# Scatters of a top-1 expert layer through 40 disjoint views of the output, and a merge that books each kind of transfer

## The chip, the core and the metric

The kernel runs on one core of a Trainium2 chip. The core has five engines that run side by side and meet only through semaphores: PE (TensorE, matrix multiplies; its weight loads are listed as PEld), DVE (VectorE), ACT (ScalarE), POOL (GpSimd) and SP (SyncE, which here only issues transfers). Each engine works through its own instruction list in order; an instruction whose semaphores are not yet there holds up everything behind it on its engine. Transfers (DMA) are issued from SP, POOL or ACT. The metric is the device time of one execution in microseconds (us), less is better.

## The reference, cut to what matters

Attention with a window of 64 positions gives `x` of 4608 tokens by 512. A gate scores each token for 8 experts; each expert takes at most 576 tokens, handed out in the order of the scores. Every expert is a two-layer product over its own tokens:

```
cap = N // E                       # 4608 // 8 = 576
for idx in order:                  # falling scores
    tok, e = (int(idx) // E, int(idx) % E)
    if assigned[tok] >= 0 or counts[e] >= cap:
        continue
    assigned[tok] = e
...
for e in range(E):
    mask = assigned == e
    h = np.maximum(x[mask] @ w1[e], 0.0)
    out[mask] = h @ w2[e]
```

Each token belongs to one expert, so each row of `out` is written once.

## The kernel before, in words

Attention comes first and stores `x` to a buffer `xs` in device memory. Then three things run together for p = 0 to 7, the p-th expert to be settled:

- **Routing** (`Routing.steps`): eight rounds on DVE and PE (line L585 counts, L512 compares) find the expert number `ei` and its threshold. Then `X`, `run`, `Y`, `A`, `B` and `R` on DVE and ACT (half of `R` is made by ACT at L722, the other half by DVE at L728) feed 18 small PE products at L734, and out of these come the token indices `idx` of expert p. Routing p runs while PE computes expert p-1.
- **Weights** (`Experts.load`): eight chunks of 512 KB per expert, four of w1 and four of w2. SP reads `ei` and issues the fetch of a chunk into one of six buffers `st` (L838). ACT rounds it to `wh` (L859) and writes `wl = -wh` (L870); a transfer issued by POOL then adds `st` onto `wl` (L872). The first three chunks of an expert are fetched as soon as `ei` is known.
- **Tokens and products**: POOL gathers the tokens (L913, five pieces `xg`), PE transposes them (L926), ACT and DVE split them into `xh` and `xl` (L903, L907). PE then makes `h` (L972), ACT and DVE turn it into `hh` and `hl` (L944, L949), and PE makes the output tiles `o` (L1004 for the last 64 tokens, L1014 for four tiles of 128). ACT evacuates each into `ot` (L986; for the last 64 tokens into `low`, L989, to which DVE adds the rest, L992), and POOL scatters `ot` to the rows of `out` (L994). There are five scatters per expert, 40 in all.

The order of the instructions on each engine is not written out by hand. `Streams` merges these generators by a simulated clock: each `yield` says how long until the generator may go on, and `busy(dt, eng)` books `dt` nanoseconds on an engine and returns when they end. Two generators that become due at different simulated times are emitted in that order, and what is emitted is the order for good: the chip keeps it on each engine, whatever the real durations are. The lines that decide where `wh` stands among ACT's other work are the estimates of a fetch:

```
SEND = 3400
LOAD = 2600
...
t = max(self.clock(), there.get(i - 1, 0)) + (LOAD if p else 1500) * (1 if i else 2)
```

So for p > 0 the first chunk of an expert is due 5200 ns after its fetch is emitted, and each further one 2600 ns later. A scatter is emitted no earlier than 3400 ns after the one before it (`self.sent + SEND`). The framework sees all scatters write the same tensor `out`, so it makes each scatter wait for the landing of the one before it.

Of the kernel before, what the change touches and what calls it, by code (L numbers as in the profile page):

```python
# [8 lines left out]

FT = mybir.dt.float32  # L10
# [12 lines left out]
E = 8  # L23
# [374 lines left out]
class Routing:  # L398


    def __init__(self, ctx, tc, c, V):
        self.tc, self.nc, self.c, self.V = tc, tc.nc, c, V
        nc = tc.nc
        rt = ctx.enter_context(tc.tile_pool(name="rt", bufs=1))
        self.rt, self.ctx = rt, ctx

        def t(name, shape, dt=FT):
            x = rt.tile(shape, dt, name=name)
            setattr(self, name, x)
            return x  # L410

        for name in ("eid", "un", "m", "best"):
            t(name, [128, NJ])
        for name in ("oh", "w", "one"):
            t(name, [128, NJ, E], BF)
        t("G0", [128, NJ, ND], BF)
        t("cw", [128, E])
        t("dg", [128, ND], I32)
        t("lane", [128, 1])
        t("rows", [128, 1], U32)  # L420
        self.setup = self.constants(c["jp"], t)
        self.idx, self.eint = {}, {}
# [367 lines left out]
STAGE = 6  # L790

GATHER = (2900, 6500)
SEND = 3400
LOAD = 2600
ADDED = 4500
FIRST = 6500

# [1 line left out]
class Experts:  # L799
    def __init__(self, ctx, tc, c, xs, w1, w2, out, ring=8):  # L800
        self.tc, self.nc, self.c = tc, tc.nc, c
        self.xs, self.w1, self.w2, self.out = xs, w1, w2, out
        self.ring = ring
        self.fw = ctx.enter_context(tc.tile_pool(name="fw", bufs=1))
        self.ps = ctx.enter_context(tc.tile_pool(name="fp", bufs=1, space=PSUM))
        self.W = {}
        self.XT = {}
        self.used = 0
        self.taken = 0
        self.first = 0  # L810
        self.gathered = 0
        self.sent = 0
        self.turned = 0
        self.tiles = [0] * E
        self.lows = [0] * E
# [10 lines left out]
    def load(self, p, ei):  # L826

        nc, fw = self.nc, self.fw
        yield lambda: self.taken == 2 * NCH * p
        e = nc.sync.value_load(ei[0:1, 0:1], min_val=0, max_val=E - 1)  # L830
        eg = nc.gpsimd.value_load(ei[0:1, 0:1], min_val=0, max_val=E - 1) if p == 0 else None
        st, there = {}, {}

        def fetch(i):
            st[i] = fw.tile([128, 1024], FT, name="st", bufs=STAGE)

            q, r = (nc.gpsimd, eg) if p == 0 and i >= 4 else (nc.sync, e)
            q.dma_start(st[i], self.part(i, r))  # L838

            t = max(self.clock(), there.get(i - 1, 0)) + (LOAD if p else 1500) * (1 if i else 2)  # L840
            if p == 0 and i == 4:

                t = max(t, self.clock() + self.busy(0, "pool") + FIRST)
            there[i] = t

        ahead = 3 if p else 4
        for i in range(ahead):
            fetch(i)
        if p == 0:
            yield lambda: self.gathered  # L850
        for i in range(2 * NCH):
            if p == 0 and i == 3:
                yield lambda: self.tiles[0] > 1
            yield lambda: self.taken - self.ring < self.used
            if there[i] > self.clock():
                yield there[i] - self.clock()
            hi = fw.tile([128, 1024], FR, name="wh", bufs=self.ring)
            lo = fw.tile([128, 1024], FR, name="wl", bufs=self.ring)
            nc.scalar.activation(hi, st[i], AF.Copy)  # L859
            yield 1050  # L860
            quick = self.quick(p, i)
            if not (p and quick):
                yield lambda: self.gathered > p
            if quick:
                nc.vector.tensor_tensor(lo, st[i], hi.bitcast(FT), OP.subtract)  # L865
                dt = self.busy(1130, "dve")
                self.spawn(self.ready(p, i, hi, lo), dt + 300 if p else 0)
            else:

                nc.scalar.activation(lo, hi.bitcast(FT), AF.Copy, scale=-1.0)  # L870
                yield 1150
                nc.gpsimd.dma_start(lo.bitcast(FT), st[i], accum_op=OP.add)  # L872
                self.spawn(self.ready(p, i, hi, lo), self.busy(650, "pool") + ADDED - 1200)
                dt = 1300
            self.taken += 1
            if i + ahead < 2 * NCH:
                fetch(i + ahead)
            yield max(100, dt - 1200) if p or i < 3 else 900
# [16 lines left out]
    def turn(self, p, idx):  # L895

        nc, fw = self.nc, self.fw
        yield lambda: self.turned == p

        def evac(a, n, t):  # L900
            r = slice(128 * a, 128 * a + n)
            t = t.bitcast(FT)
            nc.scalar.activation(xh[:, :, r], t[:, :, :n], AF.Copy)  # L903
            self.tiles[p] = a + 1
            yield 700
            self.busy(600, "dve")
            nc.vector.tensor_tensor(xl[:, :, r], t[:, :, :n], xh[:, :, r].bitcast(FT), OP.subtract)  # L907
            self.lows[p] = a + 1

        g = fw.tile([128, 5, DM], FT, name="xg")  # L910
        for a in range(5):
            n = 128 if a < 4 else 64
            nc.gpsimd.indirect_dma_start(out=g[0:n, a], out_offset=None, in_=self.xs,  # L913
                                         in_offset=IndirectOffsetOnAxis(ap=idx[0:n, a:a + 1], axis=0))
        self.gathered += 1
        there = self.clock() + self.busy(6400, "pool") + GATHER[p > 0]
        yield lambda: self.first == p
        xh = fw.tile([128, NX, CAP], FR, name="xh")
        xl = fw.tile([128, NX, CAP], FR, name="xl")
        self.XT[p] = (xh, xl)  # L920
        for a in range(5):
            n = 128 if a < 4 else 64
            yield max(0, there - 1280 * (4 - a) - self.clock())
            t = self.ps.tile([128, NX, 128], FR, name="tp", bufs=2)
            for cc in range(NX):
                nc.tensor.transpose(t[:, cc, :n], g[0:n, a, 128 * cc:128 * cc + 128].bitcast(FR), self.c["identr"][0:n, 0:n])  # L926
            dt = self.busy(300)
            self.spawn(evac(a, n, t), dt + 150)
            if p == 0 and a < 1:
                self.warm(6)  # L930
            yield dt + (1000 if p else 600)
        yield 1500
        self.turned += 1

    def steps(self, p, idx):
        nc, fw = self.nc, self.fw
# [45 lines left out]
        def put(a, o):  # L982
            ot = fw.tile([128, DM], FT, name="ot", bufs=3)
            m = 128 if a < 4 else 64
            if a < 4:
                nc.scalar.activation(ot, o, AF.Copy)  # L986
            else:
                t = fw.tile([64, DM], FT, name="low")
                nc.scalar.activation(t, o[64:128], AF.Copy)  # L989
                yield 650  # L990
                self.busy(600, "dve")
                nc.vector.tensor_tensor(ot[0:64], o[0:64], t, OP.add)  # L992
            yield max(600, self.sent + SEND - self.clock())
            nc.gpsimd.indirect_dma_start(out=self.out,  # L994
                                         out_offset=IndirectOffsetOnAxis(ap=idx[0:m, a:a + 1], axis=0),
                                         in_=ot[0:m], in_offset=None)
            self.sent = self.clock() + self.busy(1040, "pool")


        o = self.ps.tile([128, DM], FT, name="o", bufs=2)  # L1000
        for f in range(NF):
            yield lambda: (p, NCH + f // 2) in self.W
            for n, w in enumerate(self.W[p, NCH + f // 2]):
                nc.tensor.matmul(o, hh[:, f, 512:], w[:, 512 * (f % 2):512 * (f % 2) + 512],  # L1004
                                 start=(f == 0 and n == 0), stop=(f == NF - 1 and n == 1))
                yield self.busy(228)
        self.spawn(put(4, o), 100)
        for a in range(4):
            o = self.ps.tile([128, DM], FT, name="o", bufs=2)
            k = 0  # L1010
            for f in range(NF):
                wh, wl = self.W[p, NCH + f // 2]
                for wt, ht in ((wh, hh), (wl, hh), (wh, hl)):
                    nc.tensor.matmul(o, ht[:, f, 128 * a:128 * a + 128], wt[:, 512 * (f % 2):512 * (f % 2) + 512],  # L1014
                                     start=(k == 0), stop=(k == 23))
                    k += 1
                    yield self.busy(228)
            self.spawn(put(a, o), 100)
# [95 lines left out]
```

## Time and profile before

| | |
|---|---|
| median of 3 runs | 655.87 us (655.83 to 656.62) |
| the profiled execution's own time | 653.74 us |
| its span in the trace | 652.1 us |
| PE busy | 620.3 us, 95% of the span |
| weight loads busy (PEld) | 534.1 us, 82% |
| DVE, ACT, POOL busy | 447.3, 346.4, 187.6 us |

The span runs from the first to the last instruction of the program. A PE that is shown busy nearly all the time is either doing useful work or holding matmuls whose records overlap; whether it loses time is read from its waits and from the distance between the starts of its instructions. The trace belongs to one execution, which was 2.13 us quicker than the median of the timed runs.

### The profile page before, as it was taken

What the parts mean: (1) busy time and instruction counts of PE and PEld (TensorE: products, weight loads), DVE (VectorE), ACT (ScalarE), POOL (GpSimd) and SP (SyncE); (2) the same over time, 40 slices, a digit from 0 to 9 for tenths busy, and PEclk for the clock granted to TensorE, in tenths of its full rate; (3) what the DMA queues carried; (4) which work ended last, traced back from release to release, by engine and by line L of the source; (5) the groups of instructions that cost most, each with busy time, mean ns of one, the idle gap of its engine ahead of it and who ended that gap; (6) DMA issues with size and microseconds to landing.
All of it is one profiled execution on the core that took longest, in us unless ns stands there. A gap on an engine that the chain in (4) does not pass through costs nothing.

```text
span 652.1 us, 16839 instructions
## 1 busy us (share of the span) xinstructions
PE 620.3 (95%) x6383; PEld 534.1 (82%) x6383; DVE 447.3 (69%) x2102; ACT 346.4 (53%) x721; POOL 187.6 (29%) x234
## 2 busy tenths in 40 slices
PE   8999999994599999999999999999999999999996
PEld 6777778874488779978988898799889879989985
DVE  7988888887787757866885886688578754523310
ACT  6898999980254176246517624561744364424210
POOL 1333253330151062125306022430612154011011
PEclk9999999996599999999999999999999999999999
DMA  9999999921476197669739776964977599301001
GB/s 311 363 365 368 370 385 378 347 88 36 146 222 127 31 320 191 122 221 215 186 70 301 188 146 222 222 157 104 286 191 146 198 213 323 132 28 45 1 25 48
DMA packets 44656, 127.80 MB, mean 196 GB/s; under 512 B 4632, under 2 KB 5272, under 8 KB 44576
## 3 DMA queue, kind: packets, MB, share of 16 engines
q1 hardware_dynamic: 30736, 79.52, 33.9%
q0 software_dynamic: 13552, 46.69, 31.0%
q8 instruction: 50, 0.82, 0.5%
q10 hardware_dynamic: 288, 0.52, 0.3%
q14 instruction: 30, 0.25, 0.1%
HBM read 82.15 MB, written 18.87 MB: 155 GB/s over the span
## 4 chain that ended last, share of the span: by engine, by line
PE 65%; issue 5%; DVE 4%; DMA 2%; ACT 1%; POOLq 0%; ACTq 0%
PE h L972 29%; PE o L1014 26%; PE o L1004 3%; PE rps L585 2%; PE tp L926 2%; DMA st<-w 2%; PE rps L734 1%; PE rps L519 1%; DVE hl L949 1%; DMA out<-ot,idx 0%; ACT hh L944 0%; DVE run L693 0%; DVE sq L594 0%; DVE X L676 0%; DVE wl L865 0%
## 5 line engine op out<-in xcount | busy, mean ns | idle before, releaser
L994 POOL DMA_INDIRECT out<-ot,idx x40 | 42.1, 1051 | 300.2 <-DVE ot L992 110.6
L944 ACT ACTIVATE hh<-h 128x256 fp32r<-128x256 f32 (+1 forms) x128 | 52.5, 410 | 111.3 <-PE h L972 110.2
L1014 PE MATMUL o<-wh,hh 128*128 128x512 f32 x256 | 102.5, 400 | 0.0
L1014 PE MATMUL o<-wl,hh 128*128 128x512 f32 x256 | 101.8, 398 | 0.0
L1014 PE MATMUL o<-wh,hl 128*128 128x512 f32 x256 | 101.4, 396 | 0.0
L949 DVE SCALAR_TENSOR_TENSOR hl<-h,hh 128x256 fp32r<-128x256 f32 x128 | 53.4, 417 | 61.3 <-ACT hh L944 60.4
L140 ACT ACTIVATE pe<-st,mx 128x128 f32<-128x128 f32 x288 | 91.9, 393 | 5.8 <-DVE mx L135 5.5
L972 PE MATMUL h<-xh,wl 128*128 128x256 f32 (+1 forms) x512 | 93.0, 299 | 0.0
L972 PE MATMUL h<-xh,wh 128*128 128x256 f32 (+1 forms) x512 | 91.9, 299 | 0.7 <-ACT xh L903 0.7
L972 PE MATMUL h<-xl,wh 128*128 128x256 f32 (+1 forms) x512 | 92.0, 298 | 0.4 <-DVE xl L907 0.4
L972 PEld LDWEIGHTS h<-xh,wh 128*128 128x128 f32 x512 | 75.9, 189 | 1.6 <-ACT xh L903 0.8
L972 PEld LDWEIGHTS h<-xh,wl 128*128 128x128 f32 x512 | 76.1, 189 | 0.2
L972 PEld LDWEIGHTS h<-xl,wh 128*128 128x128 f32 x512 | 75.7, 190 | 0.7 <-DVE xl L907 0.6
L859 ACT ACTIVATE wh<-st 128x1024 fp32r<-128x1024 f32 x64 | 67.2, 1050 | 3.4 <-DMA st<-w 3.4
L135 DVE CUSTOM_DVE_ANT_0 st<-Sp,mask 128x128 f32<-128x128 f32 x288 | 63.8, 285 | 7.0 <-PE Sp L127 6.6
L986 ACT ACTIVATE ot<-o 128x512 f32<-128x512 f32 x32 | 19.2, 599 | 82.3 <-PE o L1014 80.9
L1014 PEld LDWEIGHTS o<-wh,hl 128*128 128x128 f32 x256 | 48.1, 188 | 9.4 <-issue 0.4
L1014 PEld LDWEIGHTS o<-wh,hh 128*128 128x128 f32 x256 | 48.2, 188 | 8.9
L1014 PEld LDWEIGHTS o<-wl,hh 128*128 128x128 f32 x256 | 48.2, 188 | 8.6
L913 POOL DMA_INDIRECT xg<-xs,idx x40 | 41.9, 1046 | 44.8 <-DVE eq L755 34.5
L870 ACT ACTIVATE wl<-wh 128x1024 fp32r<-128x1024 f32 x49 | 51.8, 1057 | 0.7
L872 POOL DMA_DIRECT2D wl<-st x49 | 45.8, 1278 | 14.5 <-ACT wl L870 14.5
(178 smaller groups left out, 1098.5 us busy)
## 6 DMA issues: line engine op xcount, KB each, us to landing
st<-w SPq DMA_DIRECT2D x60, 512.0 KB, 6.8
wl<-st POOLq DMA_DIRECT2D x49, 512.0 KB, 7.7
xs<-x SPq DMA_DIRECT2D x36, 256.0 KB, 5.1
VO<-v SPq DMA_DIRECT2D x6, 1168.0 KB, 17.8
Q<-q SPq DMA_DIRECT2D x6, 1152.0 KB, 14.1
K<-k SPq DMA_DIRECT2D x6, 1152.0 KB, 16.0
VT<-vt SPq DMA_DIRECT2D x6, 1152.0 KB, 16.0
VO<-v SPq DMA_DIRECT2D x4, 584.0 KB, 7.9
```

The lines of the kernel that those rows point to most:

```text
L135: nc.vector.tensor_tensor_reduce(st[:, h, :], Sp[h % 2][:, h // 2], mk, scale=-0.125, scalar=3.0e38, op0=OP.add, op1=OP.min, accum_out=mx[ ...
L140: nc.scalar.activation(pe[:, h, :], st[:, h, :], AF.Exp, bias=mx[:, h:h + 1], scale=-1.0)
L859: nc.scalar.activation(hi, st[i], AF.Copy)
L870: nc.scalar.activation(lo, hi.bitcast(FT), AF.Copy, scale=-1.0)
L872: nc.gpsimd.dma_start(lo.bitcast(FT), st[i], accum_op=OP.add)
L913: nc.gpsimd.indirect_dma_start(out=g[0:n, a], out_offset=None, in_=self.xs, in_offset=IndirectOffsetOnAxis(ap=idx[0:n, a:a + 1], axis=0))
L944: nc.scalar.activation(hh[:, f, c0:c1], h, AF.Relu)
L949: nc.vector.scalar_tensor_tensor(t, h[:, a - c0:b - c0], 0.0, hh[:, f, a:b].bitcast(FT), op0=OP.max, op1=OP.subtract)
L972: nc.tensor.matmul(h, wv[:, cc, 128 * (f % 2):128 * (f % 2) + 128], xt[:, cc, c0:c1], start=(k == 0), stop=(k == 11))
L994: nc.gpsimd.indirect_dma_start(out=self.out, out_offset=IndirectOffsetOnAxis(ap=idx[0:m, a:a + 1], axis=0), in_=ot[0:m], in_offset=None)
L1004: nc.tensor.matmul(o, hh[:, f, 512:], w[:, 512 * (f % 2):512 * (f % 2) + 512], start=(f == 0 and n == 0), stop=(f == NF - 1 and n == 1))
L1014: nc.tensor.matmul(o, ht[:, f, 128 * a:128 * a + 128], wt[:, 512 * (f % 2):512 * (f % 2) + 512], start=(k == 0), stop=(k == 23))
```

## The change

Three edits. The output is cut into 40 views over the same bytes, one for each scatter, which the framework takes as tensors that do not overlap, so that scatters no longer wait for one another. In the merge, the transfers become one more engine, `"dma"`: a fetch books 1350 ns (`PLAIN`), an adding transfer 2650 (`ADDING`), a gather or scatter 700 (`TOKENS`), and a transfer is due `LAND` = 2000 ns behind the end of its booking. The spacing of 3400 ns between scatters goes.

```diff
-SEND = 3400
-LOAD = 2600
+PLAIN, ADDING, TOKENS, LAND = 1350, 2650, 700, 2000
...
-        self.xs, self.w1, self.w2, self.out = xs, w1, w2, out
+        self.xs, self.w1, self.w2 = xs, w1, w2
+
+        self.out = dram_disjoint_views(out, 5 * E)
...
-            t = max(self.clock(), there.get(i - 1, 0)) + (LOAD if p else 1500) * (1 if i else 2)
+            t = self.clock() + self.busy(PLAIN, "dma") + LAND
+            if p == 0:
+                t = max(self.clock(), there.get(i - 1, 0)) + 1500 * (1 if i else 2)
...
-                self.spawn(self.ready(p, i, hi, lo), self.busy(650, "pool") + ADDED - 1200)
+                t = self.busy(650, "pool")
+                t = max(t + 350 + ADDING, self.busy(ADDING, "dma")) + LAND if p else t + ADDED - 1200
+                self.spawn(self.ready(p, i, hi, lo), t)
...
                                          in_offset=IndirectOffsetOnAxis(ap=idx[0:n, a:a + 1], axis=0))
+            self.busy(TOKENS, "dma")
...
-            yield max(600, self.sent + SEND - self.clock())
-            nc.gpsimd.indirect_dma_start(out=self.out,
+            yield max(600, self.sent - self.clock())
+            nc.gpsimd.indirect_dma_start(out=self.out[5 * p + a],
...
                                          in_=ot[0:m], in_offset=None)
+            self.busy(TOKENS, "dma")
```

`dram_disjoint_views` belongs to the framework: it returns as many handles on one tensor as it is asked for, between which no dependencies are kept.

The order of PE's and of SP's instructions stays as it was, row for row. DVE's differs only in the last two experts, where a few `wl` and `hl` of L865 and L949 change places. ACT's and POOL's change from expert 1 on. The changed kernel's line numbers are a little higher: `wh` is L863 there, `wl` L874 on ACT and L876 on POOL, `R` L723, `low` L996, `ot` L993, `hh` L951 and the scatter L1001.

POOL, during the output tiles of expert 0, behind the first three adding transfers of expert 1 (chunks 0 to 2), with the semaphores that each row waits for (DMASW: transfers issued by POOL, eight in turn; DMAHW: fetches of SP). Before:

```order
L872 DMA wl<-st 128x1024 [waits DMASW2_49,DMAHW6_49,PE_49,Activation_49]
L994 DMA out<-ot,idx_3991 4608x512 [waits DMASW7_49,DMASW3_49,Activation_49]
L994 DMA out<-ot,idx_3991 4608x512 [waits DMASW4_49,DMASW3_49,Activation_49]
L872 DMA wl<-st 128x1024 [waits DMASW5_49,DMAHW7_49,PE_49,Activation_49]
L872 DMA wl<-st 128x1024 [waits DMASW6_49,DMAHW0_49,PE_49,Activation_49]
```

And now:

```order
L1001 DMA out<-ot,idx_3991 4608x512 [waits DMASW2_49,Activation_49]
L876 DMA wl<-st 128x1024 [waits DMASW3_49,DMAHW6_49,PE_49,Activation_49]
L1001 DMA out<-ot,idx_3991 4608x512 [waits DMASW4_49,Activation_49]
L876 DMA wl<-st 128x1024 [waits DMASW5_49,DMAHW7_49,PE_49,Activation_49]
L876 DMA wl<-st 128x1024 [waits DMASW6_49,DMAHW0_49,PE_49,Activation_49]
```

Each scatter has lost the one wait that was for the scatter before it and keeps the wait for the eighth transfer back; one adding transfer now stands behind a scatter instead of ahead of it.

ACT, in the `h` products of expert 1, around the last two chunks of its weights (chunks 6 and 7). Before:

```order
L870 ACTIVATE wl<-wh 128x1024
L859 ACTIVATE wh<-st 128x1024
L944 ACTIVATE hh<-h 128x320
L870 ACTIVATE wl<-wh 128x1024
L859 ACTIVATE wh<-st 128x1024
L944 ACTIVATE hh<-h 128x320
L870 ACTIVATE wl<-wh 128x1024
L944 ACTIVATE hh<-h 128x320
```

And now:

```order
L874 ACTIVATE wl<-wh 128x1024
L951 ACTIVATE hh<-h 128x320
L863 ACTIVATE wh<-st 128x1024
L951 ACTIVATE hh<-h 128x320
L874 ACTIVATE wl<-wh 128x1024
L951 ACTIVATE hh<-h 128x320
L951 ACTIVATE hh<-h 128x256
L863 ACTIVATE wh<-st 128x1024
L874 ACTIVATE wl<-wh 128x1024
```

Chunk 6 moves behind one `hh`, chunk 7 behind two more.

ACT, where the output tiles of expert 2 begin and routing 3 ends; the `wh` is chunk 0 of expert 3. Before:

```order
L944 ACTIVATE hh<-h 128x320
L989 ACTIVATE low<-o 64x512
L722 ACTIVATE R<-A,lane 128x18x18x2
L859 ACTIVATE wh<-st 128x1024
L986 ACTIVATE ot<-o 128x512
```

And now:

```order
L951 ACTIVATE hh<-h 128x320
L996 ACTIVATE low<-o 64x512
L863 ACTIVATE wh<-st 128x1024
L723 ACTIVATE R<-A,lane 128x18x18x2
L993 ACTIVATE ot<-o 128x512
```

The same place for chunk 0 of expert 5 (and in the same way of expert 6), where `low`, `R`, `wh` stood before, now reads:

```order
L951 ACTIVATE hh<-h 128x320
L863 ACTIVATE wh<-st 128x1024
L996 ACTIVATE low<-o 64x512
L723 ACTIVATE R<-A,lane 128x18x18x2
L874 ACTIVATE wl<-wh 128x1024
```

For experts 2, 3 and 4 `wh` has moved ahead of `R` and stands behind `low`; for experts 5 and 6 it has moved ahead of `low` as well. Between the `xh` of each expert there now stand the `wh` and `wl` of its chunk 3, which stood ahead of them.

## Rows read from the trace of the kernel before

**Rows 1.** The page, busy us of each engine, share of the span, instructions.
```profile
PE 620.3 (95%) x6383; PEld 534.1 (82%) x6383; DVE 447.3 (69%) x2102; ACT 346.4 (53%) x721; POOL 187.6 (29%) x234
```

**Rows 2.** Busy us by stretch: PE, PEld, DVE, ACT, POOL, then clock, DMA.
```profile
344.12:401.23 57.11, 57.00 (x424) 50.40 (x423) 43.47 (x177) 29.57 (x48) 18.10 (x18) 1.00 0.73 193
```

**Rows 3.** PE's waits, whole span, then 240:652 us: total, times, longest us.
```profile
PE rps L734 <- ACT R L722: 2.7, 1, 2.7
PE rps L585 <- DVE G L512: 0.3, 1, 0.3
```

**Rows 4.** POOL's timeline: start, us, what, [idle before <- who ended it].
```profile
257.74 1.01 POOL L994 DMA_INDIRECT out<-ot,idx  x1 [11.57 <-DMA out<-ot,idx]
```

**Rows 5.** Chain that ended last, 246 to 262 us: start, us, what.
```profile
247.15 9.96 DMA st<-w
258.11 0.43 ACT hh L944
```

**Rows 6.** PE's timeline, 258 to 260.3 us, around the first L585 that waits.
```profile
258.80 0.40 PE L972 MATMUL h<-xh,wl 128*128 128x256 f32 x2
259.55 0.59 PE L585 MATMUL rps<-G,one 128*128 128x60 bf16 x9 [0.35 <-DVE G L512]
```

**Rows 7.** SP's timeline: fetch issue of chunk 0 of experts 2 to 6.
```profile
282.14 0.34 SPq L838 DMA_DIRECT2D st<-w  x1
339.52 0.34 SPq L838 DMA_DIRECT2D st<-w  x1
396.14 0.34 SPq L838 DMA_DIRECT2D st<-w  x1
453.20 0.34 SPq L838 DMA_DIRECT2D st<-w  x1
511.93 0.34 SPq L838 DMA_DIRECT2D st<-w  x1
```

**Rows 8.** Those fetches: size, us from issue to landing; experts 2, then 3, then 5.
```profile
st<-w SPq DMA_DIRECT2D x1, 512.0 KB, 4.0
st<-w SPq DMA_DIRECT2D x1, 512.0 KB, 3.7
st<-w SPq DMA_DIRECT2D x1, 512.0 KB, 3.6
```

**Rows 9.** ACT's timeline: expert 1's xg stage, then the end of routing 3.
```profile
237.09 1.05 ACT L859 ACTIVATE wh<-st 128x1024 fp32r<-128x1024 f32 x1
238.04 1.32 ACT L553 COPY one<-one 128x384 bf16<-128x384 bf16 x3
242.08 0.60 ACT L903 ACTIVATE xh<-tp 128x512 fp32r<-128x512 f32 x1 [0.73 <-PE tp L926]
342.19 0.90 ACT L722 ACTIVATE R<-A,lane 128x648 bf16<-128x648 bf16 x1 [2.64 <-DVE A L720]
343.24 1.06 ACT L859 ACTIVATE wh<-st 128x1024 fp32r<-128x1024 f32 x1 [0.15 <-DMA st<-w]
```

**Rows 10.** PE's timeline: first matmuls of L734, routings 2 to 6.
```profile
287.19 1.24 PE L734 MATMUL rps<-B,R 128*72 128x64 bf16 x18
343.96 1.24 PE L734 MATMUL rps<-B,R 128*72 128x64 bf16 x18
401.06 1.12 PE L734 MATMUL rps<-B,R 128*72 128x64 bf16 x16
458.79 1.24 PE L734 MATMUL rps<-B,R 128*72 128x64 bf16 x18
517.22 1.24 PE L734 MATMUL rps<-B,R 128*72 128x64 bf16 x18
```

**Rows 11.** ACT's low, DVE's ot and DVE's half of R, routing 5.
```profile
456.27 0.60 ACT L989 ACTIVATE low<-o 64x512 f32<-64x512 f32 x1 [3.91 <-PE o L1004]
456.90 0.68 DVE L992 TENSOR_TENSOR ot<-o,low 64x512 f32<-64x512 f32 x1
457.51 0.73 DVE L728 TENSOR_TENSOR R<-A,row 128x648 bf16<-128x648 bf16 x1
```

More of the change, by code (lines that the diff above doesn't have):

```diff
@@ L7 @@
 from concourse import mybir
+from concourse.ap import dram_disjoint_views
 from concourse.bass import IndirectOffsetOnAxis, ds
```

## The prediction

> **What bounds the kernel now.** I read the page first, then the stretches, then PE's waits. PE is busy 95% of the span [rows 1]. In the stretch of one expert it is busy 57.00 of 57.11 us at the full clock, 1.00, while DVE, ACT and POOL stay at 76% or less [rows 2]. PE's waits say the same from the other side: after 240 us only one wait of PE is listed, 0.3 us before a counting product of the routing [rows 3]. So from expert 1 on the kernel runs at the pace of PE's own list, and the change leaves that list as it was, row for row. It can only take away what PE still waits for, which is little, or make PE wait for something that is in time today.
>
> That PE can be made to wait for `R` is seen in routing 0, where it stood 2.7 us for ACT's `R` at L734 [rows 3]. In routings 2 to 6 it does not.
>
> **The scatters.** The wait that goes is real on POOL: one scatter of expert 0 stood 11.57 us for the landing of the one before it, with four adding transfers queued behind [rows 4]. But no wait of PE after 240 us names an adding transfer, a gather or a scatter [rows 3]. I cost the freed POOL queue at nothing; what it could give at most is the next point.
>
> **The one wait that goes.** Around 247 us the fetch of chunk 7 of expert 1 takes 9.96 us, ACT stands for it with an `hh` queued behind, which starts at 258.11 [rows 5], DVE waits for this `hh`, and the comparison for L585 stands behind it on DVE. PE shows 0.35 us idle; counted from the start of the second matmul ahead of it, since records overlap, up to 0.6 [rows 6]. In the new order chunk 6 stands one `hh` later and chunk 7 two more, so ACT does not hold these `hh` for the fetch. I take -0.5 us, between 0.35 and 0.6.
>
> **The wait that comes.** For p > 0 the first chunk of an expert was due 5.2 us after its fetch by the merge's clock; now it is due 1.35 + 2.0 = 3.35 us after. That is why `wh` of chunk 0 has moved ahead of `R` for experts 2 to 6. ACT works in order, so `R` is now late by whatever the fetch is late. The fetch goes out when `ei` is known, at the times of [rows 7], and lands 3.6 to 4.0 us later [rows 8]: later than booked. In the old order this hurt nobody: for expert 3 `R` ran at 342.19, and `wh` started at 343.24, held 0.15 us by the landing [rows 9].
>
> Now expert by expert. ACT starts `wh` 0.02 us behind the landing; an independent activation behind a `wh` starts 0.95 us after it (237.09 to 238.04), and `R` takes 0.90 [rows 9]. PE stood ready for L734 at the times of [rows 10].
>
> - Expert 3: `wh` 343.24, `R` 344.19 to 345.09, PE ready 343.96: PE waits 1.13.
> - Expert 2: landing 282.14 + 4.0 = 286.14, `R` ends 286.16 + 0.95 + 0.90 = 288.01, PE ready 287.19: 0.82.
> - Expert 4, with the 3.7 of expert 3: 396.14 + 3.7 + 0.02 + 1.85 = 401.71, PE ready 401.06: 0.65.
> - Expert 5: `wh` stands ahead of `low` too, and DVE's list has `ot` (L992), which needs `low`, ahead of its own half of `R` (L728). Today `low` takes 0.60, `ot` starts 0.03 after it, L728 starts 0.61 after that and takes 0.73 [rows 11]. `wh` 453.20 + 3.6 + 0.02 = 456.82, `low` 457.77 to 458.37, `ot` 458.40, L728 459.01 to 459.74, PE ready 458.79: 0.95.
> - Expert 6 in the same way, with 3.7: `wh` 515.65, `low` ends 517.20, L728 ends 518.57, PE ready 517.22: 1.35.
>
> Together 4.90 us. These waits add up: PE has nothing else to do in them, because its list is in order, and after each the whole rest slides, the routing of the next expert with it, so that `ei`, fetch and L734 keep their distances. Experts 1 and 7 keep `R` where it was.
>
> The Trainium skill, "DMA: Bandwidth & Descriptors", section "Anatomy of one DMA — SWDGE (gpsimd) path", fits a transfer as 2.0 us plus its bytes over 436 GB/s. For 512 KB that gives an estimate of 3.2 us, less than the trace's 3.6 to 4.0 [rows 8]; with 3.2 in all five places the waits would be 2.2 us in place of 4.9, and the time 657.6 us. The fit is for one transfer from POOL, while these fetches come from SP in bursts, so I stay with the rows.
>
> **The rest of ACT.** Chunk 3's `wh` and `wl` now stand between the `xh`. A `wh` is 1.05 us and the idle time before an `xh` is 0.73 [rows 9], so an `xh` can come up to 0.32 late, in six experts at most 1.9 us. The other bound is nothing: the transposes have two buffers and PE does other products between them. I take nothing, since PE lists no wait for `xh` after 240 us [rows 3]. The changed order of DVE in the last two experts is covered in the same way: PE lists no wait for a `wl` or an `hl` there [rows 3]; uncovered, I let it share the bound just given.
>
> **Sum.** 4.90 - 0.5 = +4.4 us. The profiled execution would go from 653.74 to 658.1 us and its span from 652.1 to 656.5. The median of the runs shown is 2.13 us above the profiled execution; I add the change to it: 655.87 + 4.4 = 660.3 us.
>
> **The rivals.** What a measurement of this kernel can tell from no change is about 0.2%, 1.3 us.
>
> - *Shorter landing.* The fetch lands as the merge books it, 3.35 us after issue. For it: the fetches of chunks 1 and 2 go out right behind the first and share its way, so 3.6 to 4.0 need not be a floor. Against: the burst is the same in the new kernel. The five waits shrink by 0.65, 0.35, 0.35, 0.25 and 0.35, to 2.95; with -0.5 the time is 658.3 us. The skill's fit, above, goes the same way, and its 657.6 us belongs to this case. Chance 0.06.
> - *Hidden after all (not slower).* PE reaches L734 later, or the fetch goes out earlier, so that `R` is in time behind `wh`. It decides at a landing 1.85 us and a little before PE's time, for expert 3 at 342.1, which is 2.6 us after issue. Nothing in rows 8 comes near. What could speak for it is a routing that gains on PE once DVE no longer waits for `hh`; against it, each of the eight rounds waits for L585 in PE's own order. It gives 655.87 - 0.5 = 655.4 us. Chance 0.07.
> - *Faster.* The early scatters and adding transfers free buffers and the DMA engines, and PE gains more than its listed waits. Everything listed after 240 us is the 0.3 to 0.6 us of above; to pass 1.3 us the distances between its matmuls would have to shrink too. 655.87 - 1.5 = 654.4 us. Chance 0.03.
> - *More waits.* The `xh` term comes in full: 4.9 + 1.9 - 0.5, 662.2 us, or more. Chance 0.04.
>
> **How the numbers follow.** The forecast, five waits of 0.6 to 1.4 us at L734 less one of 0.5, has 0.80; its own range is 659.2 to 661.6 us. Reaching to the shorter landing on one side (657.6) and to the full `xh` term on the other (662.2) leaves out the two cases at or under 655.4 and little else: 657.4 to 662.2 us. Slower has 0.80 + 0.06 + 0.04 = 0.90, within 0.2% 0.07, faster 0.03.
>
> **What would show it.** PE's waits of the changed kernel should list L734 waiting for ACT's `R` (routings 2, 3, 4) and for DVE's L728 (routings 5, 6), together near 4.9 us. ACT's timeline should show `wh` of chunk 0 ended by the landing of `st`, with `R` right behind it, and idle ACT ahead of it. The L585 near 259.5 us should have no wait, and POOL's scatters no wait for a scatter. I am wrong if L734 shows no wait, if landings fall under 3 us, or if PE's waits stand somewhere else, above all at the transposes.

## The result, and the profile after

The changed kernel takes 660.25 us (median of 6 runs, 659.17 to 661.5), the kernel before, beside it, 655.85 us (6 runs, 655.6 to 656.62). The ratio is 1.0073, with an interval of 1.0051 to 1.0094: slower by 3.3 to 6.2 us. The profiled execution took 659.17 us, with a span of 657.5 us; before it was 653.74 and 652.1.

The page of the changed kernel, busy time by engine, and from its costliest groups the rounding of weights: out and in, count, busy us and mean ns of one, idle us before and what ended it.

```profile
PE 620.2 (94%) x6383; PEld 533.5 (81%) x6383; DVE 447.9 (68%) x2102; ACT 346.0 (53%) x721; POOL 185.4 (28%) x234
...
L863 ACT ACTIVATE wh<-st 128x1024 fp32r<-128x1024 f32 x64 | 67.3, 1052 | 22.1 <-DMA st<-w 22.0
```

PE, DVE and ACT are busy for the same time as in [rows 1], within 0.6 us; PE 620.2 us where it was 620.3. So the 5.4 us between the two spans are not work: they are time in which PE stands idle. The page's one loud line is misleading about where: ACT stands 22 us for fetches ahead of `wh`. Idle time of ACT costs nothing in itself, so the question is how much of it PE sees.

PE's waits of the changed kernel, 240 to 658 us (total, times, longest, in us):

```profile
PE rps L735 <- DVE R L729: 2.8, 2, 1.5
PE rps L735 <- ACT R L723: 1.6, 3, 0.8
```

Five waits at one place, where [rows 3] has none after 240 us, and the L585 wait of 0.3 us gone. For the same time ACT's list of waits has 19.4 us at `wh`, in five pieces of up to 5.0 us, where before it had 0.8 (before, then changed):

```profile
ACT wh L859 <- DMA st<-w: 0.8, 2, 0.7
...
ACT wh L863 <- DMA st<-w: 19.4, 5, 5.0
```

PE sees 4.4 us of them.

The stretch in the middle of the span (columns as in [rows 2]):

```profile
344.00:401.00 57.00, 56.10 (x417) 49.41 (x416) 42.60 (x177) 29.07 (x46) 16.42 (x18) 1.00 0.71 187
```

PE is idle 0.90 us of 57.00, at full clock, where [rows 2] has 0.11. The five places on PE's timeline: the last product of the output tile ahead, then the first of the 18 products (start, us, what, idle before and who ended it).

```profile
287.08 0.39 PE L1022 MATMUL o<-wh,hl 128*128 128x512 f32 x1
287.85 0.89 PE L735 MATMUL rps<-B,R 128*72 128x64 bf16 x12 [0.38 <-ACT R L723]
...
344.41 0.39 PE L1022 MATMUL o<-wh,hl 128*128 128x512 f32 x1
345.59 0.65 PE L735 MATMUL rps<-B,R 128*72 128x64 bf16 x8 [0.79 <-ACT R L723]
...
402.43 0.39 PE L1022 MATMUL o<-wh,hh 128*128 128x512 f32 x1
403.29 0.89 PE L735 MATMUL rps<-B,R 128*72 128x64 bf16 x12 [0.48 <-ACT R L723]
...
460.90 0.39 PE L1022 MATMUL o<-wh,hl 128*128 128x512 f32 x1
462.59 1.24 PE L735 MATMUL rps<-B,R 128*72 128x64 bf16 x18 [1.30 <-DVE R L729]
...
520.72 0.39 PE L1022 MATMUL o<-wh,hl 128*128 128x512 f32 x1
522.65 1.24 PE L735 MATMUL rps<-B,R 128*72 128x64 bf16 x18 [1.54 <-DVE R L729]
```

The number in brackets is too small, because a record of 0.39 us overlaps the next one: where L735 does not wait, it starts 0.23 us after such a product (shown under e9 below). Counted from starts, less 0.23, PE loses 0.54, 0.95, 0.63, 1.46 and 1.70 us, together 5.28.

Why it waits is on ACT's timeline, at expert 3 and at expert 5:

```profile
339.62 0.60 ACT L996 ACTIVATE low<-o 64x512 f32<-64x512 f32 x1 [3.60 <-PE o L1012]
343.72 1.06 ACT L863 ACTIVATE wh<-st 128x1024 fp32r<-128x1024 f32 x1 [3.50 <-DMA st<-w]
344.69 0.85 ACT L723 ACTIVATE R<-A,lane 128x648 bf16<-128x648 bf16 x1
...
459.39 1.06 ACT L863 ACTIVATE wh<-st 128x1024 fp32r<-128x1024 f32 x1 [4.69 <-DMA st<-w]
460.48 0.60 ACT L996 ACTIVATE low<-o 64x512 f32<-64x512 f32 x1
460.97 0.87 ACT L723 ACTIVATE R<-A,lane 128x648 bf16<-128x648 bf16 x1
```

and on DVE's, at expert 5:

```profile
461.11 0.68 DVE L999 TENSOR_TENSOR ot<-o,low 64x512 f32<-64x512 f32 x1 [1.99 <-ACT low L996]
461.71 0.72 DVE L729 TENSOR_TENSOR R<-A,row 128x648 bf16<-128x648 bf16 x1
```

For expert 3, ACT stands 3.50 us with nothing to do but wait for the fetch, while `R` is queued behind it; in [rows 9] `R` had run at 342.19. For expert 5 the wait goes through one engine more: `low` stands behind `wh` on ACT, DVE stands 1.99 us for `low`, and its half of `R` is queued behind that.

With that the two spans can be compared: 5.28 us lost at L735, 0.66 gained near 259 us (below), and 0.79 that was there before any row changed place (the first L734 of routing 1 starts at 229.67 us before and L735 at 230.45 after; one execution against another). 5.28 - 0.66 + 0.79 = 5.4 us, and 5.4 lie between the spans.

The gain is real too. PE near 259 us, the place of [rows 6]: first the product that follows L585 there before, then the same place of the changed kernel:

```profile
259.97 0.48 PE L972 MATMUL h<-xh,wl 128*128 128x256 f32 x2
...
259.58 0.40 PE L979 MATMUL h<-xh,wl 128*128 128x256 f32 x2
259.83 0.43 PE L586 MATMUL rps<-G,one 128*128 128x60 bf16 x9
260.09 0.48 PE L979 MATMUL h<-xh,wl 128*128 128x256 f32 x2
```

No wait, and 0.25 us between the first two starts where [rows 6] has 0.75: 0.5 us. The next product starts 0.26 us after L586, where it was 0.42 after L585: 0.16 more, 0.66 together. And the scatter of [rows 4] now waits 4.04 us for its data and no longer 11.57 for another scatter:

```profile
249.90 1.05 POOL L1001 DMA_INDIRECT out<-ot,idx  x1 [4.04 <-ACT ot L993]
```

### The profile page after: what moved, and what is told of

Read it like the earlier page. It is cut to its first block, busy times and chain, and to the rows that moved or that the text cites. A ratio compares the mean times of both kernels' runs of the same rounds, so it can differ in the third digit from the quotient of the medians.

```text
span 657.5 us, 16849 instructions
## 1 busy us (share of the span) xinstructions
PE 620.2 (94%) x6383; PEld 533.5 (81%) x6383; DVE 447.9 (68%) x2102; ACT 346.0 (53%) x721; POOL 185.4 (28%) x234
## 4 chain that ended last, share of the span: by engine, by line
PE 46%; issue 19%; DVE 4%; DMA 4%; ACT 2%; POOL 1%; SPq 0%; POOLq 0%; ACTq 0%
PE h L979 21%; PE o L1022 18%; DMA st<-w 3%; PE rps L586 2%; PE tp L933 2%; PE rps L735 1%; POOL out L1001 1%; PE o L1012 1%; DMA xg<-xs,idx 1%; DVE hl L956 1%; ACT R L723 1%; ACT wh L863 0%; ACT hh L951 0%; ACT low L996 0%; DVE sq L595 0%
## 5 line engine op out<-in xcount | busy, mean ns | idle before, releaser
L1001 POOL DMA_INDIRECT out<-ot,idx x40 | 41.6, 1040 | 262.4 <-DVE ot L999 122.1
L951 ACT ACTIVATE hh<-h 128x256 fp32r<-128x256 f32 (+1 forms) x128 | 52.5, 410 | 110.2 <-PE h L979 109.1
L863 ACT ACTIVATE wh<-st 128x1024 fp32r<-128x1024 f32 x64 | 67.3, 1052 | 22.1 <-DMA st<-w 22.0
L993 ACT ACTIVATE ot<-o 128x512 f32<-128x512 f32 x32 | 19.2, 599 | 90.6 <-PE o L1022 88.6
L876 POOL DMA_DIRECT2D wl<-st x49 | 44.9, 978 | 57.3 <-ACT wl L874 37.5
L874 ACT ACTIVATE wl<-wh 128x1024 fp32r<-128x1024 f32 x49 | 51.7, 1055 | 0.5
```

What stands on the lines that cost most here:

```text
L951: nc.scalar.activation(hh[:, f, c0:c1], h, AF.Relu)
L1001: nc.gpsimd.indirect_dma_start(out=self.out[5 * p + a], out_offset=IndirectOffsetOnAxis(ap=idx[0:m, a:a + 1], axis=0), in_=ot[0:m], in_off ...
```

## The experiments

The theory: `wh` of chunk 0 stands ahead of `R` (and of `low`) on ACT and is held by a fetch that lands later than booked; PE waits for `R` at L735, five times, and apart from the half microsecond near 259 us nothing else of the change moves the time. The rivals to it were that the views or the earlier scatters cost or gain something themselves, that the other moved rows (`xh`, `hh`, chunks 6 and 7) matter, and that it is the place of `wh` that costs, its own 1 us on ACT, whatever the fetch does. The medians of the kernel before beside these runs were 656.72 us (e1, e2, e3, e5), 654.89 (e4, e6, e7, e8) and 655.24 (e9, e10).

### The two halves apart: e1_views_only, e2_merge_only

The kernel before with nothing but the 40 views:

```diff
-        self.xs, self.w1, self.w2, self.out = xs, w1, w2, out
+        self.xs, self.w1, self.w2, self.out = xs, w1, w2, dram_disjoint_views(out, 5 * E)
...
-            nc.gpsimd.indirect_dma_start(out=self.out,
+            nc.gpsimd.indirect_dma_start(out=self.out[5 * p + a],
```

> The kernel before, with only the 40 views: the order of every engine is that of before, row for row, and only the waits of scatters for scatters are gone. Theory (the loss comes from wh of chunk 0 standing ahead of R): no L734 waits after 240 us, 655.4 to 656.4 us, the same as before. Rival (earlier scatters and adding transfers collide with the fetches): a good part of the loss of 4.4 us is here already, 658 us or more.

Measured: 657.15 us, ratio 1.0009 (0.9992 to 1.0026). PE's waits, 240 to 660 us:

```profile
PE rps L586 <- DVE G L513: 0.6, 1, 0.6
PE h L973 <- ACT hh L945: 0.5, 1, 0.5
PE h L973 <- DVE hl L950: 0.4, 1, 0.4
PE tp L927 <- DVE xl L908: 0.3, 1, 0.3
```

and its POOL near 250 us:

```profile
250.03 1.01 POOL L995 DMA_INDIRECT out<-ot,idx  x1 [4.02 <-ACT ot L987]
```

The scatter is free of its 11.57 us, the time is the same as that of the kernel before beside it (656.72 us; both lie above the range expected in microseconds), the L585 wait (L586 here) is still there. That the changed kernel has no such wait comes from the merge, not from the views.

The changed kernel with one output tensor, the merge alone:

```diff
-        self.out = dram_disjoint_views(out, 5 * E)
+        self.out = out
...
-            nc.gpsimd.indirect_dma_start(out=self.out[5 * p + a],
+            nc.gpsimd.indirect_dma_start(out=self.out,
```

> The changed kernel, with one output tensor again: the order is that of the changed kernel, and scatters wait for scatters. Theory: the five waits at L734 stay, near 4.9 us together, and the time is 659.5 to 661.5 us; the POOL queue, though held up by scatters again, adds nothing since PE waits for nothing from it. Rival (the released traffic makes the loss): back to about 656 us.

Measured: 661.58 us, ratio 1.0084 (1.0067 to 1.0102). PE's waits after 215 us:

```profile
PE rps L735 <- DVE R L729: 2.5, 2, 1.5
PE rps L735 <- ACT R L723: 2.0, 3, 1.1
```

The whole loss is in the merge. The median stands 0.1 us above the range that was expected; the last section has what else was seen in this trace.

### One number of the merge: e3_first_late, e5_before_early

The changed kernel with chunk 0 booked 1850 ns later, as late as it was due before:

```diff
-            t = self.clock() + self.busy(PLAIN, "dma") + LAND
+            t = self.clock() + self.busy(PLAIN, "dma") + LAND + (1850 if i == 0 else 0)
```

> The changed kernel, with the estimate of the first chunk of an expert alone put back to 5.2 us: low, R and wh stand in the old order, everything else as in the changed kernel. Theory: all five waits at L734 go, the stall near 259 us stays away, 655.0 to 655.9 us. Rival (the rest of ACT's new order, wh and wl between the xh above all): most of the loss stays, 658 us or more.

Measured: 655.81 us, ratio 0.9996 (0.9976 to 1.0016). No wait at L735. ACT at expert 3:

```profile
342.43 0.90 ACT L723 ACTIVATE R<-A,lane 128x648 bf16<-128x648 bf16 x1 [2.63 <-DVE A L721]
...
343.43 1.06 ACT L863 ACTIVATE wh<-st 128x1024 fp32r<-128x1024 f32 x1
```

`R` is ahead again, no wait at L586 is listed either, and the loss is gone, with the views, the freed scatters and the other new bookings still in place.

The other way round, the kernel before with chunk 0 due 1850 ns earlier and chunk 1 kept where it was:

```diff
+            if p and i == 0:
+                t -= 1850
+            if p and i == 1:
+                t += 1850
```

> The kernel before, with the estimate of the first chunk of an expert alone cut to 3.35 us (the second is left where it was): low, wh and R stand as in the changed kernel, the scatters wait and are spaced as before. Theory: five waits at L734 of 4.9 us together, the stall near 259 us stays, 660.3 to 661.2 us. Rival (the views or the rest of the merge make the loss): 656 us.

Measured: 662.6 us, ratio 1.011 (1.0082 to 1.0137). PE's waits after 215 us:

```profile
PE rps L734 <- DVE R L728: 2.7, 2, 1.4
PE rps L734 <- ACT R L722: 2.1, 3, 1.0
PE rps L585 <- DVE G L512: 0.3, 1, 0.3
```

This one number makes the loss by itself. It is 5.9 us above the kernel before beside it, more than the change cost and more than was expected; the last section has what else was seen in its trace.

### The dose: e6_early_5_6, e7_early_2_4, e4_first_early

The changed kernel with chunk 0 early for experts 5 and 6 alone (e6, late for p < 5), or for 2 to 4 alone (e7, late for p > 4):

```diff
-            t = self.clock() + self.busy(PLAIN, "dma") + LAND
+            t = self.clock() + self.busy(PLAIN, "dma") + LAND + (1850 if i == 0 and p < 5 else 0)
...
+            t = self.clock() + self.busy(PLAIN, "dma") + LAND + (1850 if i == 0 and p > 4 else 0)
```

> The changed kernel, with the estimate of the first chunk put back to 5.2 us for experts 1 to 4 alone, so that wh stands ahead of low and R for experts 5 and 6 only. Theory (the waits are separate and add up): the two waits for DVE's half of R stay, 2.3 to 3.0 us together, and those for ACT's half go: 2.3 to 3.0 us over the run with all of them put back. Rival (a wait that goes is given back later): as slow as the changed kernel.

> The changed kernel, with the estimate of the first chunk put back to 5.2 us for experts 5 to 7 alone, so that wh stands ahead of R for experts 2 to 4 only, behind low. Theory: three waits for ACT's half of R, 1.9 to 2.6 us together, none for DVE's half: 1.9 to 2.6 us over the run with all of them put back. Rival as for the run with experts 5 and 6.

Measured: e6 658.03 us, ratio 1.0049 (1.0027 to 1.0071), e7 657.31 us, 1.0038 (1.0016 to 1.006). All of PE's waits after 215 us, e6, then e7:

```profile
PE rps L735 <- DVE R L729: 2.4, 2, 1.4
...
PE rps L735 <- ACT R L723: 1.8, 3, 0.7
```

The waits come and go one by one with the place of their `wh`, and each half keeps its size: 2.4 and 1.8 us here, 2.8 and 1.6 in the changed kernel. Above the kernel before the two cost 3.1 and 2.4 us, each known to within 1.4 us; together 5.6, close to the changed kernel's 4.4 to 5.5 (the second figure is e10's). So they add up, and a wait that goes is not given back later. Over e3, by the ratios, it is 3.5 and 2.7 us, a little more than expected but not clear of the noise.

The changed kernel with chunk 0 booked 1850 ns earlier still:

```diff
-            t = self.clock() + self.busy(PLAIN, "dma") + LAND
+            t = self.clock() + self.busy(PLAIN, "dma") + LAND - (1850 if i == 0 else 0)
```

> The changed kernel, with the estimate of the first chunk cut by a further 1.85 us, to 1.5 us: wh of chunk 0 now stands ahead of ot and R for expert 1 as well, and ahead of low for expert 4. Theory, worked out from the timelines of before: expert 1 adds a wait of 1.9 us at L734 (wh 229.26, ot 230.21, R 230.71 to 231.61, PE ready about 229.7); expert 4's wait grows from 0.65 to about 2.35, since low comes at 400.76 and DVE's ot stands ahead of A there. Together 3.6 us over the changed kernel: 662.5 to 665.5 us, six waits at L734. Rival (the waits at L734 only replace other lost time): no change against the changed kernel.

Measured: 669.11 us (665.4 to 670.84), ratio 1.0198 (1.0164 to 1.0231), above what was expected. PE's waits, 215 to 672 us, then two stretches of the same execution (columns as in [rows 2]):

```profile
PE rps L735 <- DVE R L729: 5.0, 3, 2.7
PE rps L735 <- ACT R L723: 3.2, 3, 2.0
```

```profile
237.50:241.50 4.00, 4.00 (x18) 3.07 (x18) 2.40 (x8) 1.09 (x2) 2.52 (x3) 0.57 0.95 338
...
413.00:419.50 6.50, 6.50 (x32) 4.80 (x30) 2.62 (x9) 1.91 (x3) 2.99 (x4) 0.54 0.48 153
```

The waits are 8.2 us where the changed kernel's are 4.4, and expert 1 has joined them. The 3.8 us more is close to the 3.6 that had been reckoned. The rest of the miss was not foreseen: a granted clock of 0.57 and 0.54 in these two stretches. Set start against start beside e8 (below), whose PE has the same list of instructions, PE falls behind by 9.1 us at the six L735 and by 4.1 us in the two stretches at the lower clock; 1.8 us it was behind already at 221 us, ahead of the first of these waits. That is 15.0 us, and the span is 15.0 us longer than e8's.

### Place or landing: e9_known_expert

In this kernel the order of PE, DVE, ACT and POOL is the changed kernel's, row for row. But chunk 0 of experts 1 to 7 is fetched from the p-th expert in storage order and not from the p-th to be settled, so its fetch needs no `ei` and SP issues it ahead of the read of `ei`. One chunk in eight of these weights is thereby another expert's; the work is the same.

```diff
+        if p:
+            first = fw.tile([128, 1024], FT, name="st", bufs=STAGE)
+            nc.sync.dma_start(first, self.w1[p, :, 0:1024])
...
+            if p and i == 0:
+                st[i] = first
+            else:
+                st[i] = fw.tile([128, 1024], FT, name="st", bufs=STAGE)
```

> The changed kernel, but chunk 0 of experts 1 to 7 is fetched from the p-th expert in storage order, without reading ei, and SP issues it ahead of that read; so this chunk of the computation uses other weights. The order of PE, DVE, ACT and POOL is that of the changed kernel, row for row, wh ahead of R included; only the landing is early. Theory (what costs is the wait of wh for its landing): no wait at L735 after 240 us, 0.999 +- 0.003 of the time before. Rival (wh ahead of R costs by its own 1.05 us of work on ACT, or by the place of low): waits of up to 1 us stay at L735, 1.004 or more.

Measured: 655.08 us, ratio 1.0 (0.9972 to 1.0028). No wait of PE is listed after 215 us. ACT at expert 3:

```profile
340.45 0.59 ACT L1001 ACTIVATE low<-o 64x512 f32<-64x512 f32 x1 [3.60 <-PE o L1017]
340.95 1.04 ACT L868 ACTIVATE wh<-st 128x1024 fp32r<-128x1024 f32 x1
...
343.69 0.89 ACT L723 ACTIVATE R<-A,lane 128x648 bf16<-128x648 bf16 x1 [1.69 <-DVE A L721]
```

and PE:

```profile
345.23 0.39 PE L1027 MATMUL o<-wh,hl 128*128 128x512 f32 x1
345.46 1.24 PE L735 MATMUL rps<-B,R 128*72 128x64 bf16 x18
```

`wh` stands ahead of `R` as in the changed kernel, but its fetch, issued at 311.21 us and landed 7.5 us later, is long done: `wh` runs right behind `low`, and ACT is free again 1.69 us before `R` can start. Of the two parts of the cause, the place and the late landing, the place alone costs nothing. It needs both.

### The stall near 259 us: e8_chunk7_late

The kernel before with the `wh` of chunk 7 of expert 1 emitted 1800 ns later, which puts the `hh` ahead of it:

```diff
+            if p == 1 and i == 7:
+                yield 1800
```

> The kernel before, with chunk 7 of expert 1 alone held back by 1.8 us of the merge's clock, so that its wh stands behind one more hh on ACT; scatters and all else as before. Theory (the stall near 259 us comes from hh queued behind a wh that waits for its fetch): this wait of PE is gone or under 0.1 us, and the time is 0.5 us below before, which the timing cannot tell from the same. Rival (DVE's routing is late there for another reason): L585 near 259.5 us still waits.

Measured: 654.68 us, ratio 1.0013 (0.9984 to 1.0041). PE near 261 us:

```profile
260.88 0.40 PE L974 MATMUL h<-xh,wl 128*128 128x256 f32 x2
261.12 0.43 PE L585 MATMUL rps<-G,one 128*128 128x60 bf16 x9
```

The wait is gone and PE has no wait left after 215 us. The cause of the stall is shown. Its half microsecond lies inside the interval, so the medians do not show its worth; the starts in the traces do. The first L734 of routing 1 starts at 229.67 us before and 231.74 in e8, that of routing 2 at 287.19 and 288.61: between the two e8's PE makes up 0.65 us, the 0.66 of the changed kernel.

### Again: e10_changed_again

The changed kernel, nothing edited.

> The changed kernel once more, for a second profile on another day of the same kernel: the five waits at L735 again, near 4.9 us in all, 1.006 to 1.009 of the time before. Open, and not part of a theory: whether the granted clock drops after the longest of these waits, near 522 us, as it did in two other kernels with this wait (e2 and e5) and did not in the first profile of this one.

Measured: 660.7 us, ratio 1.007 (1.0045 to 1.0094); waits at L735 of 2.2 us for DVE and 1.7 us for ACT, 4.7 us together by starts, less 0.23. The result repeats. This execution shows a stretch at the lower clock, told of at the end.

None of these kernels beat the kernel before: e1, e3, e8 and e9 all have 1 inside their interval.

## Why the prediction was right

**The sign and the mechanism.** PE was the bound and its list unchanged, so its waits moved the time (its clock can too, which the prediction left out; see the end), and the one that came stands where it was named: ACT's `R` for experts 2, 3 and 4, DVE's half for 5 and 6, nothing for 1 and 7. e3 takes it away by one number and e5 makes it by the same number; e6 and e7 divide it; e9 shows that it is the landing that `R` stands for. The hidden and the faster rival, and more waits at `xh`, fell with the list of PE's waits.

**The size.** The forecast was 4.90 us of waits, less 0.5, and 660.3 us; the waits came to 5.28 us by starts, less 0.66, and the median to 660.25. That the medians agree to 0.05 us is luck: the measured loss is known only to between 3.3 and 6.2 us, and e10 has 5.5. The sum of the waits is off by 0.4 us and the five terms by up to 0.5, in both directions, so that they partly cancel. The profiled execution, for which 658.1 us were forecast, took 659.17; 0.79 of that difference was there before any row changed place.

| expert | forecast, us | measured, us |
|---|---|---|
| 2 | 0.82 | 0.54 |
| 3 | 1.13 | 0.95 |
| 4 | 0.65 | 0.63 |
| 5 | 0.95 | 1.46 |
| 6 | 1.35 | 1.70 |

Experts 2 and 3 follow their landings, 3.7 and 3.5 us in this execution, where the forecast took 4.0 and 3.7 from [rows 8]. For expert 5 the landing took 3.8 and not 3.6 us; besides, `low` came 1.09 us behind the start of `wh` and not 0.95, and PE started 0.16 us after the end of L729 (461.71 + 0.72 = 462.43, and 462.59), a step that the forecast left out. These make up the 0.51 us more: `wh` started 0.23 later against the time at which PE was ready, the links up to L729's end took 0.12 more, and this last step is 0.16. Expert 6 has the same links.

**The shorter landing.** By the Trainium skill, "DMA: Bandwidth & Descriptors", section "Anatomy of one DMA — SWDGE (gpsimd) path", the estimate was 3.2 us for 512 KB. The trace disagrees: the five fetches took 3.7, 3.5, 3.7, 3.8 and 3.8 us, each with more fetches issued behind it, 0.6 us apart, and the measurement decides. The merge's booking of 3.35 us was 0.15 to 0.45 us short of what was measured.

**What was costed at nothing.** The freed scatters on POOL gave nothing (e1, between -0.8 and +2.6 in a thousand). The rest of ACT's new order, the `xh` between chunk 3's rows among it, gave nothing that e3 can tell: it keeps all of that, and is between -2.4 and +1.6 in a thousand of the kernel before. Its profile has three waits of PE of 0.3 to 0.4 us, none of them for ACT's `xh`; e1, whose order is the old one, has such small ones too.

**The -0.5 us.** The stall went, as said, and by the merge. By the starts on PE it was worth 0.66 us in the changed kernel and 0.65 in e8, a little over the 0.35 to 0.6 that the prediction allowed: the product behind L585 came earlier too. The medians can't show so small an amount.

## What to carry to other kernels

When a planner fixes an order ahead of time, an instruction that waits for a transfer should stand behind everything on its in-order engine that the critical engine needs soon, unless the transfer is sure to have landed; booking a landing a little short (here 3.35 us for 3.5 to 3.8) put it ahead of work that was in time. Read a new wait from the far end: ACT's waits for fetches grew by 18.6 us, and what it cost was the 4.4 us listed at PE. And a long wait that a change removes (11.57 us on POOL) is worth nothing until some wait of the engine that sets the pace names it.

## What was not expected of the hardware

After some waits of PE at L735 the granted clock fell. In e10 PE stood 1.22 us for `R`, and then the stretch 523 to 527 us and two starts on PE in it read:

```profile
523.00:527.00 4.00, 4.00 (x20) 2.97 (x19) 2.63 (x9) 0.00 (x0) 2.00 (x2) 0.60 0.78 295
```

```profile
524.51 0.63 PE L1022 MATMUL o<-wl,hh 128*128 128x512 f32 x1
524.93 0.63 PE L1022 MATMUL o<-wh,hl 128*128 128x512 f32 x1
```

A clock of 0.60 in the mean is a mixture of the two levels, 2.4 and 1.2 GHz; the two products start 0.42 us apart, where the changed kernel's products of the same kind keep 0.23 at a clock of 1.00 (520.49 and 520.72 on its PE), and the stretch lost about 4.00 x (1 - 0.60) = 1.6 us. e2 (0.57 in 522.00 to 525.90 us) and e5 (0.50 in 526 to 529) show the same after the wait of expert 6, and e4 twice, after waits of 2.01 and 2.72 us. But the changed kernel's first profile shows 1.00 in the same stretch after a wait of 1.54 us, and e6 after one of 1.44. So the wait's length alone does not decide it, and what does stays open. In all twelve traces, the two kernels' and the ten runs', the clock between 185 us and the last 6 us of the span is 1.00 but for these five falls; no trace without a wait at L735 (L734) there has one. Such a fall would explain why some executions of e2, e5 and e10 are 1 to 2 us longer than their waits; that each of them had one is not shown. The same holds for the changed kernel itself: its profiled execution was the quickest of the six, at a mean granted clock of 0.981 over the span, and the other five have 0.975 to 0.977. Whether one of these falls is part of their time was not seen, so the median's 4.4 us may hold some of it beside the waits.
